# A PSUM-to-SBUF cast of the query projection moved from VectorE to ScalarE in a recurrent attention kernel

## The chip, the cores and the metric

The kernel runs on one core of one Trainium2 chip. The metric is the device time of one execution in microseconds (us); lower is better. A core has five engines that run side by side and wait for one another on semaphores: TensorE (PE; its weight loads have a row of their own, PEld), VectorE (DVE), ScalarE (ACT), GpSimd (POOL) and SyncE (SP). Each works through its own instructions in program order.

## The reference

Two layers A and B are applied twice to a sequence of 2048 rows of width 512, each after a layer norm and with a residual sum. The change lies in A, attention over short segments with a memory that is carried from one to the next:

```python
for s in range(n_seg):                       # 64 segments of 32 rows
    xs = x[:, s * seg_len:(s + 1) * seg_len, :].copy()
    h = jnp.concatenate([mem, xs], axis=1)   # 8 memory rows + 32 rows
    q = jnp.einsum('btd,dhe->bhte', h, Wq)   # 32 heads of 128
    k = jnp.einsum('btd,dhe->bhte', h, Wk)
    v = jnp.einsum('btd,dhe->bhte', h, Wv)
    scores = jnp.einsum('bhqe,bhke->bhqk', q, k) * scale
    scores = jnp.where(mask[None, None], scores, -1000000000.0)
    p = _softmax(scores, axis=-1)
    o = jnp.einsum('bhqk,bhke->bhqe', p, v)
    o = jnp.einsum('bhte,hed->btd', o, Wo)
    mem = o[:, :M, :].copy()
    outs.append(o[:, M:, :])
```

Segment s+1 needs the memory that segment s has put out, so the 64 segments of a block A follow one another. Two blocks A make 128 segments. B is a gated MLP with a 2048 x 2048 mixing over the rows.

## The kernel before, in words

`a_block` runs one A and `b_block` one B; in time they are A, B, A, B. In `a_block` the order of work on TensorE, VectorE and ScalarE is the order in which the code issues it (`manual_schedule` for these three), and the semaphores are derived from which instruction reads and writes what.

`segment(s, ...)` issues one segment. Of the 40 rows of `h` it projects 32 at once: the 8 new memory rows and 24 of the segment's rows, which lie transposed in `hT`. The remaining 8 rows of each segment, which do not depend on the memory, are projected four segments at a time beside it (`b_units`, tiles `psb`, with ScalarE copies at L768 and L775), as filler for TensorE. `y_part` is a second kind of filler, tiles `pwB`, which multiplies earlier outputs by `Wo`; its results are added on VectorE at L830 or copied at L836. `tb` is a group of four segments and `j4` the segment in the group.

A segment's 32 heads come in two halves r of 16. `qk(j, ps, copy)` makes one projection chunk: j = 0 and 1 are the queries of the two halves, 2 and 3 the keys. It issues 16 matmuls into a PSUM tile (L714), takes a `[P, 512]` bf16 buffer from the pool `rowsQK`, which has three buffers, and copies the PSUM result into it (L925), splitting the elements into even and odd ones. The copy is a cast from fp32 to bf16; the engine that runs it is the argument `copy`, ScalarE if not given. `qk_T` then transposes that buffer on VectorE into `QQ` (queries) or `KA` (keys) (L928). The order in a segment is:

- query half 0 into `psQ[:, 0]`, then key half 0 into `psQ[:, 1]`, the other PSUM bank of the same tile, then both transposes;
- query half 1 into `psm` and its transpose;
- key half 1 into `psK[:, 0]`; a quarter of the value projection (`psK[:, 1]`);
- `scores(0)` (L951, L955) into `psS`, then on ScalarE `exps(0)` (L960), then on VectorE the transpose of key half 1;
- the rest of the value projections (`psK`, `psV`), with `scores(1)` and `exps(1)` between them; on VectorE the masks (`close`, L963) and the copy of the values (L1049);
- the sums for the softmax (`sums_zero`, `sums_tokens`), the products with the values (`pv`, L1000), the memory rows' outputs (`memory_out`, L1021), the product with `Wo` (L794, L801), the new memory, transposed into the next segment's `hT` (L900), and at last the outputs of the other rows (`tok_out` L1024, `last_out` L1027), after ScalarE has worked out their reciprocals (L1097, L1100).

VectorE issues four instructions of `tok_out` and `last_out`, and in some segments an addition (L830), a copy (L836) or a half of a residual sum (`y_half`, L249), before it comes to the next segment's first query. ScalarE issues L1100, and in some segments copies of `b_units`, before it comes to the next segment's keys. `other_bank(mms, read)` tells the dependency tracker that the matmuls into one bank need not wait for the copy out of the other.

Of the kernel before, what the change touches and what calls it, by code (L numbers as in the profile page):

```python
# [581 lines left out]
def qk_rhs(w, j, kt, cg):  # L582
    return w[j // 2][:, kt, :].rearrange("p (r gs i eb el) -> p r eb i gs el", r=2, gs=4, i=4, eb=4)[:, j % 2, cg]
# [86 lines left out]
def a_block(tc, c, rows, front, MV_in, RS_in, MV_out, RS_out, ahead, wo, S, first):  # L670
    nc = tc.nc
# [5 lines left out]
    with ExitStack() as ctx:  # L677
# [34 lines left out]
        def mm_chunk(ps, lhs, rhs, kts=range(KT)):  # L712

            return [nc.tensor.matmul(ps[32 * cg:32 * cg + 32, :], lhsT=lhs(kt, cg), rhs=rhs(kt, cg), start=(kt == 0), stop=(kt == KT - 1),  # L714
                                     tile_position=(0, 32 * cg)) for kt in kts for cg in range(4)]
# [192 lines left out]
        def segment(s, fill, spare1, spare2, spare3, tail, loads):  # L908
# [13 lines left out]
            def qk(j, ps, copy=nc.scalar.copy):  # L922
                mms = mm_chunk(ps, lambda kt, cg: hA_cur[:, kt, :], lambda kt, cg: qk_rhs(w, j, kt, cg))
                r = rowp.tile([P, 512], BF16, name="rows", tag="rowsQK", bufs=3)
                return r, mms, copy(r[:].rearrange("p (n el two) -> p n el two", n=8, two=2), ps.rearrange("p (n two el) -> p n el two", n=8, two=2))  # L925
# [102 lines left out]

            begin = first and s == 0
            psQ = att.tile([P, 2, 512], F32, name="psQ")  # L1030
            r0, _, read = qk(0, psQ[:, 0, :], nc.vector.tensor_copy)
            r2, mms, _ = qk(2, psQ[:, 1, :])
            other_bank(mms, read)
            qk_T(0, r0)
# [1 line left out]
            r1, _, _ = qk(1, accB.tile([P, 512], F32, name="psm")[:])  # L1036
            qk_T(1, r1)
            psK = attO[0].tile([P, 2, 512], F32, name="psK")
            r3, _, read = qk(3, psK[:, 0, :])
# [116 lines left out]
        for s in range(NSEG):  # L1156
# [78 lines left out]
            def loads():  # L1235
                if due and s < NSEG - 1 and (not ys or tb == NB - 1):
# [7 lines left out]
                    else:  # L1244
                        y_load(y, wo.VX[0][:].rearrange("p j r e -> p (j r e)").bitcast(F32))

            segment(s, lambda n=1: [next(more, None) for _ in range(n)], spare1, spare2, spare3, tail, loads)
        assert due == [NB - 5] and ys == [[NB - 6, True]]
        for k in range(3):
# [57 lines left out]
```

## Time and profile before

| | |
|---|---|
| median of 3 runs | 1655.38 us (1653.51 to 1658.37) |
| the profiled execution | 1654.03 us, span 1652.3 us from its first to its last instruction |
| mean granted TensorE clock | 0.996 |
| first block A / first B | about 30 to 694 us / 694 to 850 us |
| second block A / second B | about 850 to 1503 us / 1503 to 1652 us |
| DMA | 148.96 MB moved, 90 GB/s on average |

A row of a group or a timeline reads: source line, engine, operation, `output<-input`, partitions x elements and type, and how many instructions were merged into the row (`x16`). In brackets stands the idle time of the engine just before, and which instruction ended it. The weight loads of TensorE (PEld) run ahead of its matmuls; matmuls are pipelined, so their rows overlap, and the end of one is modelled. Two VectorE or ScalarE instructions in a row overlap in the records too, the next one starting before the last one's row ends.

The busiest engine changes little over the block: in the first block A, 29.8 to 850 us with its B, TensorE is busy for 793.7 of 820.2 us, VectorE for 586.1 and ScalarE for 493.4.

### The profile page before, as it was taken

The numbers are of one execution on the slowest core, as the hardware profiler recorded it, in microseconds if no ns is written. First come the engines' busy times: TensorE is split into PE (matmuls) and PEld (weight loads), VectorE is DVE, ScalarE is ACT, GpSimd is POOL, SyncE is SP. The second block draws the span as 40 slices with busy tenths as digits, with TensorE's granted clock in tenths as the row PEclk, the third lists the DMA queues.
The fourth block names the chain that finished last, engine by engine and source line by source line (L and its number), as shares of the span: only waits on it lengthen the run. The fifth ranks groups of instructions, "written<-read, shape, count | busy, mean of one in ns | idle before, by whom it ended". The sixth has DMA issues, their size and how long they took to land.

```text
span 1652.3 us, 90089 instructions
## 1 busy us (share of the span) xinstructions
PE 1589.0 (96%) x40647; PEld 966.1 (58%) x40670; DVE 1151.6 (70%) x3180; ACT 976.7 (59%) x2153; POOL 288.0 (17%) x604
## 2 busy tenths in 40 slices
PE   5899999999999999899999999999999999998999
PEld 2465556665665556566655555566556566554565
DVE  4677777777777787784467777777787777777722
ACT  2576766666666666561036677666666666665400
POOL 5111111112211221320011111111121112223000
PEclk8999999999999999999999999999999999999999
DMA  9322111113321333277952211122332223425696
GB/s 363 86 42 47 42 42 42 42 43 83 80 46 42 85 81 79 90 175 148 217 160 48 46 47 46 46 47 46 74 88 69 47 70 93 95 52 151 151 201 157
DMA packets 263609, 148.96 MB, mean 90 GB/s; under 512 B 197560, under 2 KB 239648, under 8 KB 263224
## 3 DMA queue, kind: packets, MB, share of 16 engines
q1 hardware_dynamic: 249992, 99.38, 27.3%
q0 software_dynamic: 13232, 43.82, 8.1%
q8 instruction: 318, 5.21, 1.3%
q14 instruction: 67, 0.55, 0.1%
HBM read 59.68 MB, written 37.19 MB: 59 GB/s over the span
## 4 chain that ended last, share of the span: by engine, by line
PE 49%; DVE 4%; ACT 4%; issue 1%; DMA 0%; ACTq 0%; DVEq 0%
PE pg L397 9%; PE psK L714 5%; PE psQ L714 5%; PE psb L714 5%; PE pz L296 5%; PE px L794 4%; PE psV L714 3%; PE psm L714 2%; PE psO L801 2%; PE py L440 2%; PE psO L1000 1%; ACT rows L925 1%; DVE uT L1024 1%; PE psT L992 1%; ACT Rt L1097 1%; PE psS L951 1%
## 5 line engine op out<-in xcount | busy, mean ns | idle before, releaser
L714 PEld LDWEIGHTS <-hT 128*32 128x32 bf16 x12288 | 334.4, 97 | 282.5 <-DVE hT L900 15.9
L714 PE MATMUL psV<-Wv_sb,hT 128*32 128x512 bf16 x2048 | 165.3, 379 | 0.0
L1024 DVE TENSOR_TENSOR uT<-psO,Rt 128x384 bf16<-128x384 f32 x256 | 140.4, 548 | 31.1 <-ACT Rt L1100 30.9
L1021 DVE TENSOR_TENSOR uT<-psO,Rm 128x128 bf16<-128x128 f32 x256 | 74.6, 291 | 124.9 <-ACT Rm L1018 123.4
L925 ACT CAST rows<-psQ 128x512 bf16<-128x512 f32 x128 | 74.9, 585 | 146.0 <-DVE rows L925 131.5
L397 PE MATMUL pg<-z,wspT 128*128 128x344 bf16 x1024 | 154.3, 309 | 0.0
L714 PE MATMUL psK<-Wv_sb,hT 128*32 128x512 bf16 x2048 | 153.9, 378 | 0.0
L960 ACT ACTIVATE S<-psS 128x224 bf16<-128x224 f32 x256 | 91.9, 359 | 102.7 <-PE psS L955 102.7
L928 DVE STREAM_TRANSPOSE KA<-rows 128x256 f32<-128x256 f32 x256 | 114.0, 445 | 54.0 <-ACT rows L925 51.2
L1100 ACT ACTIVATE Rt<-Rt 128x512 f32<-128x512 f32 x256 | 147.2, 622 | 4.1
L714 PE MATMUL psQ<-Wq_sb,hT 128*32 128x512 bf16 x2048 | 135.4, 381 | 12.6 <-DVE hT L900 8.4
L794 PEld LDWEIGHTS <-uT 128*32 128x32 bf16 x4608 | 122.7, 97 | 33.4 <-DVE uT L1021 3.6
L714 PE MATMUL psQ<-Wk_sb,hT 128*32 128x512 bf16 x2048 | 136.9, 383 | 0.2 <-issue 0.2
L714 PE MATMUL psm<-Wq_sb,hT 128*32 128x512 bf16 x2048 | 136.4, 383 | 0.0
L794 PE MATMUL px<-Wo,uT 128*32 128x256 bf16 x3840 | 133.9, 273 | 1.5 <-issue 0.2
L714 PE MATMUL psK<-Wk_sb,hT 128*32 128x512 bf16 x2048 | 134.8, 379 | 0.0
L1097 ACT ACTIVATE Rt<-psT 128x1024 f32<-128x1024 f32 x128 | 131.1, 1024 | 3.1
L885 POOL COPY KX<-old 128x128 bf16<-128x128 bf16 x128 | 67.4, 526 | 370.5 <-PE psS L955 249.1
L397 PEld LDWEIGHTS <-wspT 128*128 128x128 bf16 x1024 | 100.2, 98 | 53.2
L885 POOL COPY KX<-front 128x128 bf16<-128x128 bf16 x126 | 64.7, 520 | 357.5 <-PE psS L955 203.1
L801 PE MATMUL psO<-Wo_high,uT 128*32 128x128 bf16 x7168 | 124.2, 219 | 1.2 <-issue 1.2
L928 DVE STREAM_TRANSPOSE QQ<-rows 128x256 f32<-128x256 f32 x256 | 114.1, 446 | 13.0 <-ACT rows L925 2.7
(201 smaller groups left out, 2988.6 us busy)
## 6 DMA issues: line engine op xcount, KB each, us to landing
o_d<-o_sb SPq DMA_DIRECT2D x126, 64.0 KB
vb_d<-front SPq DMA_DIRECT2D x30, 256.0 KB
VX<-vb_d SPq DMA_DIRECT2D x120, 64.0 KB
ln_x<-xd SPq DMA_DIRECT2D x26, 256.0 KB
y_o<-o_d POOLq DMA_DIRECT2D x22, 256.0 KB, 3.3
xd<-y_o POOLq DMA_DIRECT2D x22, 256.0 KB, 2.8
Wq_sb<-in_A_Wq_dram POOLq DMA_DIRECT2D x8, 512.0 KB, 9.2
Wk_sb<-in_A_Wk_dram POOLq DMA_DIRECT2D x8, 512.0 KB, 10.4
```

Source lines behind the costliest of these rows:

```text
L296: nc.tensor.matmul(pz[:, c0:c1], lhsT=xnT[:, kt, :], rhs=w_in_sb[:, kt, c0:c1], start=(kt == 0), stop=(kt == KT - 1))
L397: nc.tensor.matmul(pg[t][:, k, 0:344], lhsT=wsp[t][:, st, :], rhs=z(st, 344 * k, 344 * k + 344), start=(st == 0), stop=(st == NT - 1))
L714: return [nc.tensor.matmul(ps[32 * cg:32 * cg + 32, :], lhsT=lhs(kt, cg), rhs=rhs(kt, cg), start=(kt == 0), stop=(kt == KT - 1), tile_posi ...
L794: nc.tensor.matmul(px[at:at + 32, 0:256], lhsT=lhs[:, h, :], rhs=wo_rhs(h, slice(k + 2, None, -2) if h % 2 else slice(k, None, 2)), start= ...
L801: nc.tensor.matmul(pw[32 * cg:32 * cg + 32, :], lhsT=lhs[:, h, :], rhs=wo_rhs(h, cg), start=False, stop=(h == H - 1), tile_position=(0, 32 ...
L885: eng.tensor_copy(KX[:, :, r].rearrange("p g (k i) -> p i g k", i=4), bs["KTB"][:, r].rearrange("p (i g) k -> p i g k", i=4)[:, :, :, 8 * ...
L925: return r, mms, copy(r[:].rearrange("p (n el two) -> p n el two", n=8, two=2), ps.rearrange("p (n two el) -> p n el two", n=8, two=2))
L928: nc.vector.transpose(out=(QQ[:, j % 2, :, 0:32] if j < 2 else KA[:, j % 2]).bitcast(F32).rearrange("p n q one -> p n (q one)"), in_=r[:]. ...
L960: return nc.scalar.activation(out=S[:, r], in_=psS[:, r, 0:224], func=ACT.Exp, scale=scale)
L1024: nc.vector.tensor_tensor(out=hview(uT_nxt[:], r, 0, 24), in0=oview(r, 8, 32), in1=rview(r, 0, 24), op=ALU.mult)
L1097: nc.scalar.activation(out=Rt[:], in_=psT[:], func=ACT.Ln)
L1100: nc.scalar.activation(out=rt, in_=rt, func=ACT.Exp, scale=-1.0)
```

## The change

The first query chunk of each segment is copied by the default engine of `qk`, ScalarE, instead of VectorE:

```diff
             begin = first and s == 0
             psQ = att.tile([P, 2, 512], F32, name="psQ")
-            r0, _, read = qk(0, psQ[:, 0, :], nc.vector.tensor_copy)
+            r0, _, read = qk(0, psQ[:, 0, :])
             r2, mms, _ = qk(2, psQ[:, 1, :])
             other_bank(mms, read)
             qk_T(0, r0)
             qk_T(2, r2)
```

VectorE loses one instruction a segment, 128 in all. ScalarE's order gains 128, each ahead of the cast of key half 0. The orders on TensorE, GpSimd and SyncE are the same as before.

## The prediction

> **What bounds the kernel now.** I read the page's table of engines first, then the waits of the weight loads, then the timeline of single segments. The table names TensorE:
>
> ```profile
> PE 1589.0 (96%) x40647; PEld 966.1 (58%) x40670; DVE 1151.6 (70%) x3180; ACT 976.7 (59%) x2153; POOL 288.0 (17%) x604
> ```
>
> The longest wait of the weight loads (line waited for: us, times, longest) shows where that stream stands still all the same:
>
> ```profile
> PEld L951 <- DVE KA L928: 77.7, 190, 2.3
> ```
>
> L951 is the scores, once per half r and segment; they wait for the transposes at L928, which wait for the casts at L925. The rows of the tile `rows` show what these cost and who waits for whom (ns as min/median/max, then us and times):
>
> ```profile
> L928 DVE STREAM_TRANSPOSE KA<-rows x256: 397/446/448, 34.1 to 1503.9; 128x256 f32<-128x256 f32 x128
> L925 DVE CAST rows<-psQ x128: 677/680/693, 31.8 to 1501.5; 128x512 bf16<-128x512 f32 x128
> L925 ACT CAST rows<-psQ x128: 585/585/587, 33.5 to 1502.3; 128x512 bf16<-128x512 f32 x128
>   ACT rows L925: 131.5, 122
> ```
>
> The last line: in 122 of 128 segments ScalarE sat idle until VectorE had finished its cast, 131.5 us in all. The timeline of segment 24 of the first block shows why that reaches TensorE (start, us, instruction, idle before):
>
> ```profile
> 283.79 1.07 PE L714 MATMUL psQ<-Wq_sb,hT 128*32 128x512 bf16 x16
> ...
> 285.49 0.68 DVE L830 TENSOR_TENSOR yB<-pwB,yB 128x512 f32<-128x512 f32 x1
> ...
> 286.09 0.68 DVE L925 CAST rows<-psQ 128x512 bf16<-128x512 f32 x1
> ...
> 286.86 0.58 ACT L925 CAST rows<-psQ 128x512 bf16<-128x512 f32 x1 [2.21 <-DVE rows L925]
> ...
> 287.48 0.45 DVE L928 STREAM_TRANSPOSE KA<-rows 128x256 f32<-128x256 f32 x1 [0.23 <-ACT rows L925]
> ...
> 287.98 0.28 PE L951 MATMUL psS<-QQ,KA 128*32 128x40 bf16 x16 [0.32 <-ACT rows L925]
> ...
> 289.20 0.27 PE L951 MATMUL psS<-QQ,KA 128*32 128x40 bf16 x16
> ```
>
> Times below count from a segment's first psQ matmul, here 283.79. VectorE reaches its cast at 2.30, ScalarE follows at 3.07, the first scores start at 4.19 and the second at 5.41. Compare segment 23, where VectorE has no L830:
>
> ```profile
> 273.75 1.04 PE L714 MATMUL psQ<-Wq_sb,hT 128*32 128x512 bf16 x16
> ...
> 275.46 0.68 DVE L925 CAST rows<-psQ 128x512 bf16<-128x512 f32 x1
> ...
> 276.23 0.58 ACT L925 CAST rows<-psQ 128x512 bf16<-128x512 f32 x1 [0.66 <-DVE rows L925]
> ...
> 277.42 0.27 PE L951 MATMUL psS<-QQ,KA 128*32 128x40 bf16 x16
> ...
> 278.63 0.26 PE L951 MATMUL psS<-QQ,KA 128*32 128x40 bf16 x16
> ```
>
> Scores start at 3.67 and 4.88. Two facts from going through all segments. First, 3.67 is TensorE's own floor: where the key transpose ended as early as 3.19 to 3.34 the scores still began at 3.67. The second scores follow 1.21 to 1.22 later, or 0.07 after the last transpose if that is later. Second, everything behind the second scores is rigid: the first L1021 comes 1.73 to 1.88 after them in every segment from the second on. So a segment is as long as its second scores are late: 10.57 us from segment 24 to 25 with 5.41, 10.03 from 21 to 22 with 4.88.
>
> **The change part by part.** In each of 128 segments it removes VectorE's 0.68 us cast, with it ScalarE's wait, and puts a cast of the same shape ahead of ScalarE's three. The trace has no ScalarE cast of that half, but has the other half of the same tile at 585 ns; I take that. No DMA, matmul or POOL instruction moves. On ScalarE the new cast can delay the key cast, the two behind it and the first Exp (L960).
>
> The casts' new starts: a projection can be cast 1.09 us after its first matmul (the psK cast starts at 3.68 where it waits for TensorE, its matmuls at 2.59), so 1.09, 1.95, 2.82 and 3.68 for the four. Queued ScalarE casts start 0.48 apart (286.86, 287.34, 287.82). A transpose starts 0.04 after its cast ends, or 0.49 after the transpose before. From these and the measured ends of each engine's earlier work:
>
> - 58 segments as number 23. ScalarE is free at about 1.8, so casts at 1.72, 2.20, 2.82, 3.68; the key transpose ends at 3.28 instead of 3.54. TensorE's floor hides it: 0. Without that floor the 0.26 would show.
> - 24 segments as number 24 (VectorE held by L830 or L836, ScalarE idle since about 0.85). Casts at 1.09, 1.95, 2.82, 3.68, transposes at 2.30, 2.79, 3.44, 4.30; scores at 3.67 and 4.89, before 5.41: 24 x -0.52 = -12.5 us.
> - 14 segments where VectorE is held by a half addition (L249) and ScalarE by a copy until 2.23. Casts at 2.13, 2.61, 3.09, 3.68, key transpose done 3.70, scores 3.75 and 4.97, before 5.37: 14 x -0.40 = -5.6 us.
> - 13 segments with ScalarE busy to about 2.2 and VectorE free at 1.87. The same casts, and now the scores at 3.75 instead of 3.68: up to 0.07 lost in ten of them, +0.7 us; the other three about even. This is the change's own cost.
> - 11 segments with neither engine held much (second scores near 5.03): 11 x -0.15 = -1.6 us.
> - The last two segments of each block: VectorE reaches its cast at 3.16 (segment 62), second scores at 6.28; after, transposes from 3.04, second scores 5.25: 4 x -1.0 = -4.1 us. Two more lose 0.1 each: -0.2. The two first segments wait for TensorE: 0.
>
> Sum: -12.5 - 5.6 + 0.7 - 1.6 - 4.1 - 0.2 = -23.3 us. The profiled execution took 1654.0 us (span 1652.3), 1.4 under the median of the three runs, so 1630.7 against it, or 1632 in terms of the median.
>
> The new cast's bounds: if ScalarE's casts did not overlap at all (585 ns apart), the 13 and the 14 segments would give +2.6 and -2.8 and the sum -18; with 45 ns of dead time between them as well, -14. On the other side a cast costing nothing would add some 2 us in the 14 and spare the 0.7, about -26. I take the 0.48 that the rows show.
>
> One rule speaks for the dearer end: the Trainium skill, Advanced Engine Details and Errata, section The Read-Write Bubble, says that ScalarE and VectorE pay the memory latency between instructions, since accesses are not pipelined from one to the next. By that the sum would be -18; the rows, 585 ns long and 0.48 apart, contradict it here.
>
> **The rivals.**
>
> *TensorE is full, so nothing changes.* For it: 96% busy, and matmul rows idle only 17.9 us before L951. Earlier scores would then be swallowed by the matmuls behind them: 1655 us. Against it: segments 24 and 21 run the same projections and scores, and differ by 0.53 us exactly where the scores do. The Trainium skill, Perfetto Trace Analysis, section Identifying the Most-Contended Engine, calls matmul busy time a poor measure and weight-load busy time the better one; at 58% it leaves room.
>
> *The new cast starts only when VectorE is free.* In the changed program it carries, in most segments, a VectorE wait besides TensorE's, as a buffer of `rows` must be free. If the instruction waited for were VectorE's latest, the 24 would gain 0.13 instead of 0.52, the 14 the same 0.13, the last four 0.26, the 11 0.13; with the +0.7 of the 13 together -6.6 us, 1649. Against it: with three buffers and four tiles a segment the buffer was last read by a transpose of the segment before.
>
> *Slower: the key cast waits for the query transpose.* It too carries a VectorE wait. If that were for the transpose just issued, the cast would start 0.06 after it ended: in the 58 at 2.85, key transpose done 3.92, second scores 0.28 to 0.31 later (+16.5); the 13 lose 0.65 (+8.4), the 14 0.25 (+3.5); the 24 keep -0.25 (-5.9), the rest -2.9. Together about +19.5, 1675 us. It decides once the key cast starts later than about 2.5 in the 58. Against it: it is the fourth cast, not the second, that reuses the first one's buffer.
>
> That the change does not do what it says is out: 128 casts have left VectorE's order and stand first among ScalarE's, and the other engines' orders are the same.
>
> **How the numbers follow.** Forecast 0.78; new cast bound to VectorE 0.09; no change 0.07; slower 0.06. Against this kernel's runs (0.3% from lowest to highest) a change of 0.3%, 5 us, can be told from none. The forecast's own range is 1625 to 1642, from the bounds above with a few us for the runs' spread; with the second case it reaches 1650. Faster 0.87, same 0.07, slower 0.06.
>
> **What would show it.** Right: no VectorE cast at L925; no ScalarE idle time until VectorE there; the waits of L951 for KA down from 77.7 us to some 25, what stays being the last transpose's; scores at 3.67 and 4.88 in segment 24; 0.05 to 0.10 longer segments of the 13. Wrong: second scores of segment 24 earlier but L1021 not, or weight loads waiting longer elsewhere, or first scores past 3.8 in segments like 23.

## The result and the profile after

The changed kernel takes 1628.15 us (median of 4 runs, 1627.71 to 1629.33) against 1654.45 of the kernel before: ratio 0.9843, 95% interval 0.9817 to 0.9868, some 26 us less. Two later comparisons on other occasions gave 0.9848 (0.9828 to 0.9869) and 0.9833 (0.9816 to 0.9849). The profiled execution has a span of 1626.3 us.

The page's engine row, and the two longest waits of the weight loads (line waited for: us, times, longest):

```profile
PE 1579.0 (97%) x40647; PEld 976.1 (60%) x40670; DVE 1065.8 (66%) x3052; ACT 1047.4 (64%) x2281; POOL 290.4 (18%) x604
```

```profile
PEld L1000 <- DVE VA L1049: 52.4, 128, 0.4
PEld L951 <- DVE KA L928: 39.5, 154, 0.8
```

VectorE has lost 86 us of work, ScalarE gained 71. The scores' wait for the key transposes went from 77.7 us to 39.5, and its longest from 2.3 to 0.8. The wait for the copied values (L1000, 52.4 us) now leads the list; it was 52.5 us before.

The rows of the tile `rows`, first the casts (ns as min/median/max), then for what their engines sat idle, then who waited for them:

```profile
L925 ACT CAST rows<-psQ x256: 567/596/611, 31.4 to 1474.6; 128x512 bf16<-128x512 f32 x128
...
  ACT rows L925: 126.3, 304
  PE psK L714: 28.0, 101
  PE psQ L714: 22.7, 71
...
  ACT rows L925: 0.8, 2
```

The VectorE cast is gone, 256 ScalarE casts of `psQ` stand where there were 128, and ScalarE's idle time until VectorE fell from 131.5 us to 0.8. What ScalarE waits for now is TensorE. VectorE waits for ScalarE longer than before, 126.3 us against 53.9; the second scores below show that this costs little.

Segment 24 of the first block, whose lines before are in the prediction:

```profile
281.18 1.08 PE L714 MATMUL psQ<-Wq_sb,hT 128*32 128x512 bf16 x16
...
282.30 0.58 ACT L925 CAST rows<-psQ 128x512 bf16<-128x512 f32 x1 [0.30 <-PE psQ L714]
282.84 0.68 DVE L830 TENSOR_TENSOR yB<-pwB,yB 128x512 f32<-128x512 f32 x1
283.16 0.58 ACT L925 CAST rows<-psQ 128x512 bf16<-128x512 f32 x1 [0.28 <-PE psQ L714]
283.44 0.43 DVE L928 STREAM_TRANSPOSE QQ<-rows 128x256 f32<-128x256 f32 x1
...
283.80 0.43 DVE L928 STREAM_TRANSPOSE KA<-rows 128x256 f32<-128x256 f32 x1
...
284.85 0.28 PE L951 MATMUL psS<-QQ,KA 128*32 128x40 bf16 x12
...
286.06 0.28 PE L951 MATMUL psS<-QQ,KA 128*32 128x40 bf16 x12
```

Counted from the segment's first matmul, the two psQ casts start at 1.12 and 1.98, each as soon as TensorE has its half ready, while VectorE has L830 still ahead of it or under way. The key transpose is done at 3.05 instead of 4.14, and the scores start at 3.67 and 4.88 instead of 4.19 and 5.41. The segment takes 10.06 us instead of 10.57.

Taken over all 128 segments, the second scores' start within the segment changed as follows (sums in us over the segments of a kind, against the first profile of before; changed, again and third are the three profiles of the changed kernel, the other names are those of the next section):

| kind, segments | forecast | changed | again | third | e1 | e2 | e3 | e4 | e6 |
|---|---|---|---|---|---|---|---|---|---|
| TensorE's floor, 58 | 0 | +0.1 | -0.3 | 0.0 | -0.4 | +0.2 | -0.2 | +7.7 | +18.9 |
| ScalarE late, 13 | +0.7 | +0.5 | +0.6 | +0.4 | -0.6 | -0.3 | +0.4 | +6.9 | +9.3 |
| VectorE late, 24 | -12.5 | -12.7 | -12.5 | -12.7 | -8.0 | -12.5 | +0.2 | -12.6 | -5.5 |
| both late, 14 | -5.6 | -5.8 | -5.8 | -5.6 | -4.8 | -5.6 | -0.2 | +1.1 | +3.8 |
| light, 11 | -1.6 | -1.6 | -1.7 | -1.7 | -1.6 | -1.6 | +0.2 | -1.7 | -1.6 |
| last two of a block, 4 | -4.1 | -5.4 | -4.8 | -3.8 | -1.3 | -3.6 | 0.0 | -4.8 | -1.5 |
| two small ones, 2 | -0.2 | -0.2 | -0.2 | -0.1 | -0.1 | -0.1 | +0.3 | +0.2 | +1.0 |
| first of a block, 2 | 0 | -2.5 | +0.1 | -1.9 | -1.5 | -1.7 | -2.2 | -2.6 | -0.3 |

The last row varies from profile to profile of one kernel (1.3 us between the two of before), as shown below.

### The profile page after: what moved, and what is told of

Its sections match the earlier page's. It is cut to its first block, busy times and chain, and to the rows that moved or that the text cites. A ratio compares the mean times of both kernels' runs of the same rounds, so it can differ in the third digit from the quotient of the medians.

```text
span 1626.3 us, 90252 instructions
## 1 busy us (share of the span) xinstructions
PE 1579.0 (97%) x40647; PEld 976.1 (60%) x40670; DVE 1065.8 (66%) x3052; ACT 1047.4 (64%) x2281; POOL 290.4 (18%) x604
## 3 DMA queue, kind: packets, MB, share of 16 engines
q8 instruction: 318, 5.21, 1.3%
## 4 chain that ended last, share of the span: by engine, by line
PE 53%; DVE 2%; DMA 1%; issue 1%; POOL 1%; ACT 0%; POOLq 0%; SPq 0%
PE pg L397 9%; PE psQ L714 7%; PE psK L714 7%; PE psb L714 5%; PE px L794 4%; PE psm L714 3%; PE psV L714 3%; PE psO L801 3%; PE pz L296 3%; PE py L440 2%; PE pwB L813 1%; PE psO L1000 1%; PE psT L992 1%; PE psS L951 1%; PE psS L974 0%
## 5 line engine op out<-in xcount | busy, mean ns | idle before, releaser
L714 PEld LDWEIGHTS <-hT 128*32 128x32 bf16 x12288 | 338.5, 97 | 274.1 <-DVE hT L900 13.3
L925 ACT CAST rows<-psQ 128x512 bf16<-128x512 f32 x256 | 142.8, 594 | 23.3 <-PE psQ L714 22.7
```

## The experiments

All edits are against the changed kernel. Three theories are told apart. *Lateness*: a segment is as long as its second scores are late, and the change helps where VectorE came late to its transposes. *The wait*: the cost was ScalarE's idling for VectorE's cast. *The load*: each segment gains because VectorE has 0.68 us less to do.

**e1: the wait alone taken out.**

```diff
-            r0, _, read = qk(0, psQ[:, 0, :])
-            r2, mms, _ = qk(2, psQ[:, 1, :])
-            other_bank(mms, read)
+            r0, _, read = qk(0, psQ[:, 0, :], nc.vector.tensor_copy)
+            r2, mms, key = qk(2, psQ[:, 1, :])
+            other_bank(mms + [key], read)
```

> The first query cast is back on VectorE, but ScalarE's key cast is declared free of VectorE's query cast, so only the wait is taken out and VectorE keeps its 0.68 us. Theory of lateness (a segment is as long as its second scores are late, and those are late because VectorE comes late to its transposes): part of the gain, about -16 us against before: -7.7 in the 24 segments where VectorE has L830 or L836 (second scores near 5.09 instead of 5.41), -4.5 in the 14 with L249 and ScalarE busy, -1.8 in the last four, -1.7 in the 11 light ones, none in the 58 and the 13. Theory of the wait (ScalarE's 131.5 us of idle time is the whole cost): all of it, -26. Theory of the load (each segment gains from 0.68 us less on VectorE): about 0.

Measured: 0.9882 of before (0.9867 to 0.9896), -19.5 us. The timeline of segment 24:

```profile
281.62 1.04 PE L714 MATMUL psQ<-Wq_sb,hT 128*32 128x512 bf16 x16
...
283.57 0.59 ACT L925 CAST rows<-psQ 128x512 bf16<-128x512 f32 x1 [1.09 <-PE psQ L714]
283.92 0.68 DVE L925 CAST rows<-psQ 128x512 bf16<-128x512 f32 x1
...
284.64 0.45 DVE L928 STREAM_TRANSPOSE QQ<-rows 128x256 f32<-128x256 f32 x1
285.01 0.40 DVE L928 STREAM_TRANSPOSE KA<-rows 128x256 f32<-128x256 f32 x1
...
285.46 0.28 PE L951 MATMUL psS<-QQ,KA 128*32 128x40 bf16 x16
...
286.69 0.27 PE L951 MATMUL psS<-QQ,KA 128*32 128x40 bf16 x16
```

ScalarE now casts the keys at 1.95, ahead of VectorE's cast at 2.30, yet VectorE's own 0.68 us still hold the transposes: second scores at 5.07, between 5.41 and 4.88. So the change has two parts. Without the wait some 17 to 22 of its 26 us come back; the rest, mainly in the 24 and the last four segments, needs the cast off VectorE.

**e2 and e3: the change by kinds of segment.** In e2 ScalarE has the cast in the 55 segments that were forecast to gain, in e3 in the other 73 (`LATE` lists the segments by block). The expectations count 57 and 71, but the kinds that they name add up to 55 (24, 14, 11, 4 and 2), and so do the lists of the edit; the trace of e2 has 73 VectorE casts, that of e3 55. By load the two would be -11 and -15 us.

```diff
+LATE = {True: {1, 2, 3, 4, 8, 12, 16, *range(20, 64, 4), 35, 37, 39, 41, 51, 53, 55, 57, 61, 62, 63},
+        False: {4, 8, 12, 16, *range(20, 64, 4), 35, 37, 39, 41, 51, 53, 55, 57, 61, 62, 63}}
-            r0, _, read = qk(0, psQ[:, 0, :])
+            r0, _, read = qk(0, psQ[:, 0, :], nc.scalar.copy if s in LATE[first] else nc.vector.tensor_copy)
```

> The first query cast runs on ScalarE only in the 57 segments of the kinds that should gain (24, 14, 11, the last four of the blocks, and the two small ones, with segment 35 of each block among the 14), on VectorE in the other 71. Lateness: the whole gain, -25 us against before, within 2 us of the changed kernel. Load: 57 of 128 parts of 26 us, -12.

> The reverse: on ScalarE in the 71 segments that TensorE's own floor should cover, on VectorE in the 57. Lateness: +0.6 us against before (the 13 with late ScalarE), so no change that can be told. Load: 71 of 128 parts of 26 us, -14.

Measured: e2 0.9834 (0.9819 to 0.9848), -27 us; e3 0.9988 (0.9978 to 0.9997), -2 us. All the gain lies in the 55, and the load theory is out in both. That e3 is not slightly slower but 0.5 to 3.6 us faster is not explained by the second scores of its segments (+0.7 without the first of each block); it stays open, and is about the size of the spread of a kernel's runs.

**e4: the new cast done twice.**

```diff
+            again = rowp.tile([P, 512], BF16, name="again", bufs=1)
+            read2 = nc.scalar.copy(again[:].rearrange(...), psQ[:, 0, :].rearrange(...))
             r2, mms, _ = qk(2, psQ[:, 1, :])
-            other_bank(mms, read)
+            other_bank(mms, read, read2)
```

> The changed kernel, with the first query cast done twice on ScalarE in each segment (the second time into a buffer that nothing reads), ahead of the key cast: 128 more casts of 0.585 us. Lateness: the key transpose comes 0.48 later where ScalarE was busy before; 58 segments lose 0.11, 13 lose 0.46, 14 lose 0.47, the rest nothing, so +19 us against the changed kernel, -5 to -8 against before. If ScalarE's spare time hides such a cast: as the changed kernel, -26. If each cast costs its own 0.48 on the path: +61 against the changed kernel.

Measured: 0.9959 (0.9946 to 0.9972), -6.8 us against before, so about 19 to 20 us dearer than the changed kernel. Segment 23, a kind that TensorE's floor covers:

```profile
276.09 1.04 PE L714 MATMUL psQ<-Wq_sb,hT 128*32 128x512 bf16 x16
...
277.80 0.60 ACT L925 CAST rows<-psQ 128x512 bf16<-128x512 f32 x1
278.27 0.61 ACT L1033 CAST again<-psQ 128x512 bf16<-128x512 f32 x1
...
278.75 0.62 ACT L925 CAST rows<-psQ 128x512 bf16<-128x512 f32 x1
...
279.90 0.28 PE L951 MATMUL psS<-QQ,KA 128*32 128x40 bf16 x16
...
281.12 0.27 PE L951 MATMUL psS<-QQ,KA 128*32 128x40 bf16 x16
```

The key cast starts 0.95 after the first query's, so the scores start at 3.81 and 5.03: of the 0.48 us the floor hides 0.33, and 0.15 show. The 24 and the 11, where ScalarE was idle, lose nothing (-12.6 and -1.7 stand). The same extra cast costs 0, 0.13 or 0.5 us depending on the segment: cover is a quantity that can be used up.

**e6: the slower rival, made on purpose.** The first two casts share one buffer, the other two have two.

```diff
-                r = rowp.tile([P, 512], BF16, name="rows", tag="rowsQK", bufs=3)
+                r = rowp.tile([P, 512], BF16, name="rows", tag=f"rowsQK{j % 4 in (1, 3)}", bufs=1 + j % 2)
```

> The changed kernel with one buffer shared by the first query's and the first key's cast, so that the key cast must wait for the query's transpose: the slower rival of the prediction, made on purpose. Its price there: +19.5 us against before (58 segments +0.28, 13 +0.65, 14 +0.25, 24 -0.25), that is some +43 against the changed kernel. If a wait there is hidden by TensorE's floor: as the changed kernel.

Measured: 1.0146 of before (1.0122 to 1.0169), +24 us. Segment 23:

```profile
278.24 1.04 PE L714 MATMUL psQ<-Wq_sb,hT 128*32 128x512 bf16 x16
...
280.58 0.45 DVE L928 STREAM_TRANSPOSE QQ<-rows 128x256 f32<-128x256 f32 x1 [0.55 <-ACT rows L925]
...
281.12 0.59 ACT L925 CAST rows<-psQ 128x512 bf16<-128x512 f32 x1 [0.57 <-DVE QQ L928]
...
282.23 0.28 PE L951 MATMUL psS<-QQ,KA 128*32 128x40 bf16 x16 [0.15 <-ACT rows L925]
...
283.45 0.27 PE L951 MATMUL psS<-QQ,KA 128*32 128x40 bf16 x16
```

The key cast stands at 2.88 and waits 0.57 us for the query's transpose; second scores at 5.21, +0.33 against 4.88. The rival was a mechanism that could have been there, at somewhat more than its forecast price of +19.5 (interval 20 to 28 us). In the changed kernel the key cast has a buffer of its own and does not wait.

**e5: two buffers instead of three** (`bufs=2` in the same line).

> The changed kernel with two buffers for the four casts instead of three, so that the second query's cast waits for the first query's transpose and the second key's for the first key's. By the measured ends (2.79 and 3.28 in the 58, against starts at 2.82 and 3.68) both waits lie under TensorE's: no change, within 2 us of the changed kernel. If waits on transposes cost in themselves, as they do where the first key's cast waits: 10 us or more.

Measured: 0.9839 (0.9819 to 0.9859, two runs), beside 0.9833 of the changed kernel on the same occasion: no difference that can be told. So two buffers already keep the slower rival out: the fault of e6 is that its two casts share one. A buffer wait costs only where it binds.

**e7: the best of each kind.** As e2, and in the other 73 segments VectorE's cast without the wait, as in e1. It ran twice, each time beside the changed kernel; the last two expectations are for the latter.

```diff
+            late = s in LATE[first]
+            r0, _, read = qk(0, psQ[:, 0, :], nc.scalar.copy if late else nc.vector.tensor_copy)
+            r2, mms, key = qk(2, psQ[:, 1, :])
+            other_bank(mms if late else mms + [key], read)
```

> ScalarE casts the first query only in the 57 segments where VectorE comes late or ScalarE is idle; in the other 71 VectorE keeps the cast, and ScalarE's key cast does not wait for it. This takes away the 0.06 that the 13 segments with late ScalarE pay: -0.5 to -1 us against the changed kernel, too little to tell by the times, visible in the second scores of those segments (4.89 instead of 4.96). If ScalarE's load in the 71 costs anything else, more than 2 us.

> The mixed kernel again, to see whether its 2.7 us under the changed kernel (medians 1624.05 and 1626.79, intervals overlapping) hold. The second scores of the 13 explain about 1.2 us, so I expect 0.5 to 2 us, and the intervals to overlap again. If the 2.7 us hold with intervals apart, ScalarE's load in the 71 costs something that the second scores do not show.

> The changed kernel once more, beside the next two. Lateness, with the first segments' clock taken as chance: 1.5% under before, as measured first (0.9843).

> The changed kernel, beside the next one: near 0.9845 of before.

Measured: medians 1624.05 and 1626.79 (changed kernel) the first time, 1625.13 and 1624.96 the second. The second scores of the 13 are earlier as expected (-0.6 and -0.3 in sum, against +0.5, +0.6 and +0.4 in the changed kernel's profiles), but the times cannot tell the two kernels apart: the first 2.7 us were spread.

**The kernel before once more**, for its first segments.

> The kernel before once more, for a second profile. If the half clock at the start of the second block's first segment (granted clock 0.63 there, 1.00 in all five later profiles) is chance, this profile shows about 1.00 and a span near 1650.5; if it belongs to the kernel, 0.63 again and 1652.

The granted clock in the 3.5 us from the first matmul of the second block's first segment, in before and then in the changed kernel (the column ahead of the last two):

```profile
850.06:853.56 3.50, 3.50 (x43) 1.67 (x47) 1.91 (x4) 1.08 (x3) 0.25 (x1) 0.62 0.50 177
```

```profile
835.17:838.67 3.50, 3.50 (x68) 1.98 (x72) 1.72 (x5) 2.14 (x5) 0.26 (x1) 1.00 0.53 182
```

The second profile of before gave 0.53 with a span of 1650.7, so neither expectation held as written: the half clock came back and the span was still lower. The changed kernel's second profile settles that it does not belong to the kernel before: its clock there was 0.57 too, with a span of 1621.4, and 1.00 in the third. The half clock costs 1.7 us in that segment (11.72 us against 10.03) and fell on before but not on the changed kernel in the first pair of profiles. With what the first block's first segment lost (0.8 us, its clock 0.50 against 0.56), that is the table's -2.5. Both profiles of before have the half clock and one of three of the changed kernel; so few do not show whether it is equally likely in both, and up to 1.7 of the 26 us could come from it.

## Why the prediction was right

**The bound.** Right: with TensorE at 96% before and 97% after, the time went down by 26 us. The rival in which TensorE is full fell; a high busy share left room for the scores to come earlier. e2 and e3 show it segment by segment: the gain is where the second scores were late and nowhere else.

**The 24 segments.** Forecast -12.5, measured -12.7, -12.5 and -12.7, by the mechanism named: the median starts of the casts are 1.09, 1.95, 2.82 and 3.68, and the scores stand at TensorE's floor.

**The 14 and the 13.** Forecast -5.6 and +0.7, measured -5.8 and +0.5. The 0.48 us between queued ScalarE casts was the right choice; by 0.585 the 13 would have lost 2.6. (The sum by that price is -18.6 from its own terms, where the prediction writes -18.) The Trainium skill, Advanced Engine Details and Errata, section The Read-Write Bubble, puts the memory latency between one instruction and the next. Taken as the prediction priced it, as rows that cannot overlap, that does not hold for these casts, 585 ns long and 0.48 us apart; a shorter gap inside the 0.48 us could not be told from these rows. L249, which holds VectorE in the 14, is the normalisation of a block of rows (`y_norm`, row `ln_xn<-y_o,MV,RS`) and not the half of a residual sum that it is called further up; the term rests on when it ends, and stands.

**The 58 and the 11.** Forecast 0 and -1.6, measured +0.1 and -1.6. e4 measured the cover that the first of these terms rested on.

**The last four segments.** Right in kind, mis-sized: forecast -4.1, measured -5.4, -4.8 and -3.8. The prediction let transposes follow one another at 0.49 us. That distance was taken from rows of before in which each transpose waited for a cast, and the casts were 0.48 apart. Where the casts are done early, as in segment 62 after, it is less:

```profile
669.93 0.43 DVE L928 STREAM_TRANSPOSE QQ<-rows 128x256 f32<-128x256 f32 x1
...
670.30 0.39 DVE L928 STREAM_TRANSPOSE KA<-rows 128x256 f32<-128x256 f32 x1
670.54 0.54 POOL L224 DMA_DIRECT2D rowsB<-o_d  x1 [1.42 <-ACT rows L925]
670.57 0.58 ACT L925 CAST rows<-psK 128x512 bf16<-128x512 f32 x1 [0.28 <-PE psK L714]
670.62 0.39 DVE L928 STREAM_TRANSPOSE QQ<-rows 128x256 f32<-128x256 f32 x1
```

0.37 and 0.32 apart. In the second profile, where VectorE comes to these segments as it did before, that makes the key transpose end some 0.18 us earlier than forecast, which is the -4.8. The other two hold chance besides: in the first VectorE came to the work ahead of its transposes 0.1 to 0.3 us sooner in three of the four segments, and in the third one normalisation took 1.55 us instead of 0.55, in the last segment of the second block:

```profile
1472.15 1.55 DVE L249 TENSOR_SCALAR ln_xn<-y_o,MV,RS 128x512 bf16<-128x512 f32 x1
```

Why it did is not known; without it the third profile would have some -4.8 too.

**The sum.** Without the first segment of each block the second scores of the three profiles are 25.3, 24.6 and 23.5 us earlier in sum, where the forecast had 23.3. The times fell by 26, 25 and 28 us in the three comparisons, so the forecast is a little low (the interval of the third begins at 25). Of what lies outside these scores the forecast counted nothing: the first segments, and the time from the second scores to the next segment's first matmul. The latter, summed over the other segments of the blocks A, is 642.9 and 641.6 us in the two profiles of before and 644.8, 639.0 and 640.9 in the three of the changed kernel. So it is rigid in most segments but not in the sum, and one kernel's profiles differ in it by up to 5.8 us; why was not followed up.

**The rival of the cast that waits for VectorE** (1649 us) fell: ScalarE waited 0.8 us for VectorE in all.

**What would show it.** The scores at 3.67 and 4.88 in segment 24 came true. In eight of the 13 the second scores came 0.05 to 0.06 us later, at the low end of the 0.05 to 0.10 named. The wait of L951 for the key transposes did not fall to some 25 us but to 39.5. Of these, 27.3 us are the second scores' weights, which wait 0.16 to 0.24 us in nearly every segment, as they did in the 58 before; that is what the prediction expected to stay. The other 12.1 are the first scores', mostly in the 13 and the 14, where ScalarE is late; these it did not count.

## What to carry to other kernels

A long in-order chain with a fixed tail can be costed by one instant in each period, here the start of the second scores; sort the periods by which engine comes late to it, and cost each kind by its own queue. Where two engines take turns at one stage, ask both what the second one waits for and what the first one still has queued: taking the wait out gave some two thirds to four fifths of the gain, moving the work the rest. Cover has a size: TensorE's floor hid one cast more on ScalarE, and not two.

## What the runs showed of the hardware that was not expected

VectorE transposes of 128x256 fp32, 445 ns long in most rows and 390 to 430 ns where they follow one another, start 0.32 to 0.37 us apart when nothing holds them; ScalarE casts of 585 ns start 0.48 apart. So a row's length is not what it costs in a queue.

TensorE started the second block's first segment at a granted clock of 0.53 to 0.62 over its first 3.5 us in four of the thirteen profiles (in the first of before it is 0.50 from 1.0 to 4.0 us) and at 1.00 in nine. In the first profiles of before and of the changed kernel, one of each sort, TensorE's matmuls had been idle for the same 2.5 us ahead of it. The Trainium skill, TensorE: Matmul & The Clock Gate, Part 1, says that the clock is halved after at least one idle window of about 3.4 us, and that the windows run freely. 2.5 us without matmuls cannot fill such a window, so by these words the clock would have stayed; in four profiles it did not, and the measurement decides. Why the same idle time halves it in some profiles and not in others is not shown.

The sum of the weight loads' waits is no measure of time: the scores' weights waited 53.0 us for the key transposes in e2 and 39.5 in the changed kernel, which is not faster.
